# Loading padded head pairs as full 128-row tiles, with weight splits, gate transposes and the last counts in other places

## The chip, the core and the metric

The kernel runs on one core of a Trainium2 chip. A core has five engines with instruction streams of their own: TensorE (PE, matrix products; its weight loads are shown as PEld), VectorE (DVE), ScalarE (ACT), GpSimd (POOL) and SyncE (SP, which here issues DMAs), and sixteen DMA engines that move data between the device's memory and the core's on-chip memory of 128 rows (partitions). Each engine runs its instructions in order and waits where an operand or a buffer is not ready. The metric is the device time of one execution in microseconds; smaller is better.

## The reference

Two layers follow each other. The first is a gated recurrent attention (mLSTM) over 4 batches, 8 heads, 768 time steps and a head size of 40. The second is a mixture of experts: each of the 3072 tokens goes to one of 8 experts, a two-layer product of width 1024.

```python
for t in range(S):
    m_new = np.maximum(f_gate[:, :, t] + m, i_gate[:, :, t])
    f_stab = np.exp(f_gate[:, :, t] + m - m_new)
    i_stab = np.exp(i_gate[:, :, t] - m_new)
    m = m_new
    C = f_stab * C + i_stab * outer(vt, kt)
    n = f_stab * n + i_stab * kt
    h_tilde, nq = C @ qt, n . qt
    y[:, :, t] = sigmoid(o_gate) * h_tilde / max(abs(nq), 1)

logits = x @ w_gate                     # x: y as 3072 tokens of 320
expert_idx = np.argmax(logits, axis=1)  # and its softmax weight gate_w
for e in range(E):                      # the tokens of expert e
    out[mask] = gate_w[mask] * (np.maximum(x[mask] @ w1[e], 0) @ w2[e])
```

## The kernel before

**Items and steps.** The time axis is cut into 6 chunks of 128. An item is one chunk of one batch with its 8 heads: 24 items, numbered chunk by chunk (item = 4 * chunk + batch). The program is written as a hand-made order (`manual_schedule`): `start()`, then `step(s)` for s = 0 to 23, then `end()`, then the experts. Every engine runs its instructions in the order in which this code issues them. Nothing is re-ordered by a scheduler; the places of the calls set the queues.

**An attention item.** In a chunk the recurrence becomes matrix products. `scores` multiplies keys and queries (PE, L290). `spread` broadcasts the running maximum `mparts` over rows with the selector `sel` (PE, L246). `decay` makes the decay matrix `dd` on ACT (L258, eight exponentials), and POOL zeroes its upper half. `pmul` multiplies scores and decay into `pp` on DVE (L297). `attend` does the products with values: with the carried state `cz` (L310, from chunk 1 on), with `pp` (L313) and the update of the state (L317). `gated` multiplies by the sigmoid of the output gate `sg` into `yT` (DVE, L326; ACT makes the sigmoid of a whole chunk of all batches in one instruction, L212). `natural` turns `yT` to tokens in rows, together with the router's logits (PE, L345). `finish` divides and leaves the tokens `xs` (DVE, L355 to L374), and `store` writes them to device memory. `weigh_k` and `weigh_q` scale keys and queries on POOL (`kw`, `qg`), and `factors` spreads the gate factors (PE L234, ACT copy `gb` L239). In step s stand `scores(s)`, the preparation of items s+1 and s+2, `natural` and `finish` of item s-2, and `attend(s-1)`.

**Heads in rows.** Two heads share a tile of keys and queries (`tq`) or output gates (`sg`): one in rows 0 to 39, the other in rows 64 to 103. `load_t` and `load_og` fill such a tile with two DMAs of 48 rows (40 of data and 8 of padding), at rows 0 and 64. Instructions that work on all of rows 0 to 104 read the rows between as well, so POOL zeroes rows 32 to 63 of the six tiles once (L679, L708). `tq` has four buffers and is loaded three steps ahead, `sg` two.

**Gates.** The gates of all items are scanned at the start in two groups: `gt[0]` for chunks 0 to 3, `gt[1]` for chunks 4 and 5. `flip` transposes `a` (PE L193, copied by ACT to `aT`), `flip_w` makes the weights `w` (ACT, L198), transposes them (PE, L199) and copies them (`wT`). `parts` splits an f32 array in three bf16 pieces for `mparts` or `gparts`. For `gt[1]` the scan is in step 2, `carry` in step 3, the two transposes in step 4.

**Clock.** `stir` issues products of a zero tile on PE whose result nobody reads.

**Routing.** When a group of 4 or 2 items has its logits, `choose` takes the expert (DVE), `count` adds up positions with matrix products (PE, L413 to L415) in `pos_ps`, a part of the PSUM bank `x_ps` in which `natural` writes as well, `total` counts an expert's tokens (L461), `seen` reads them, `share` and `place` give weight and slot, and POOL scatters the tokens to expert lists with indirect DMAs.

**Weights.** The f32 weights of an expert come in 7 chunks, by `pull` into four buffers `raw`; `high` (ACT, L522) rounds a chunk and `low` (DVE, L526) makes the remainder. `split` does both. `SPLITS` says how many chunks are split in which step of the attention part for the first expert. `third` transposes gathered tokens (PE L561, ACT L562, DVE L564), `first` and `second` are the two layers (L576, L599).

## Time and profile before

| | |
|---|---|
| median of the runs shown | 406.84 us (404.06 to 408.29, 3 runs) |
| the profiled execution's own time | 404.99 us |
| its span, first to last instruction | 403.1 us |
| mean granted PE clock | 0.911 of full speed |
| busy: PE / PEld / DVE / ACT / POOL | 364.1 / 332.2 / 248.9 / 200.4 / 164.3 us |
| DMA | 59.01 MB, 146 GB/s over the span |
| attention part, about | 0 to 170 us |

A row of the timeline reads: start, length (us), engine, line and operation, out<-in with the shape, number of instructions merged, and in brackets the idle time of the engine before it with what ended it. Line numbers are those of the kernel before. SPq and ACTq are DMA issues. A row of the windows view has the length of the stretch, the busy time of each engine in it with the number of instructions, the granted clock of PE, the mean busy share of the sixteen DMA engines (over 1 where packets overlap) and GB/s. A row of DMA issues has the number of issues, KB of each and the median us from issue to landing.

### The profile page before, as it was taken

How to read it: one execution, taken by the hardware profiler on the slowest of the kernel's cores; microseconds unless marked ns; L12 is line 12 of the kernel's file. 1: busy time of each engine (PE TensorE's matmuls, PEld its weight loads, DVE VectorE, ACT ScalarE, POOL GpSimd, SP SyncE). 2: the span in 40 equal slices, each digit the busy share in tenths (PEclk: the TensorE clock that was granted, in tenths of full speed). 3: DMA queues.
4: the chain of work that ended last, by engine and by line, in shares of the span. 5: the costliest groups of instructions: out<-in, count | busy, mean ns of one | idle time of the engine just before them, and what ended most of it. 6: DMA issues, size and time to landing. Idle time of an engine off the chain costs nothing. (4 is left out here: it accounts for less than half of the span.)

```text
span 403.1 us, 8943 instructions
## 1 busy us (share of the span) xinstructions
PE 364.1 (90%) x3256; PEld 332.2 (82%) x3257; DVE 248.9 (62%) x625; ACT 200.4 (50%) x447; POOL 164.3 (41%) x214
## 2 busy tenths in 40 slices
PE   7788689999999987787799999999999999999970
PEld 3567678999988876687698898899999999989970
DVE  3879697999997997665352733935735556373300
ACT  3697556677765950034343533543535546454310
POOL 4726354787887575512415025014023132122020
PEclk9659696999999696589699999999999999999996
DMA  8985857798969952070742354354454545641000
GB/s 195 249 200 156 194 124 179 131 251 179 222 197 239 270 127 84 1 221 19 248 155 80 94 173 139 91 182 120 135 182 129 173 135 183 180 141 32 10 24 11
DMA packets 31535, 59.01 MB, mean 146 GB/s; under 512 B 8916, under 2 KB 20637, under 8 KB 30914
## 3 DMA queue, kind: packets, MB, share of 16 engines
q1 hardware_dynamic: 27810, 49.93, 47.8%
q0 software_dynamic: 3456, 8.36, 6.7%
q8 instruction: 26, 0.43, 0.5%
q10 hardware_dynamic: 224, 0.15, 0.1%
q14 instruction: 19, 0.16, 0.1%
HBM read 50.17 MB, written 8.70 MB: 146 GB/s over the span
## 5 line engine op out<-in xcount | busy, mean ns | idle before, releaser
L604 POOL DMA_INDIRECT out<-y,ls x24 | 23.7, 989 | 119.4 <-ACT y L603 109.1
L599 PE MATMUL bank<-w2h,hh 128*128 128x320 f32 (+1 forms) x224 | 71.1, 317 | 0.0
L586 DVE SCALAR_TENSOR_TENSOR hl<-bank,hh 128x256 fp32r<-128x256 f32 (+4 forms) x72 | 39.2, 549 | 51.4 <-ACT hh L585 50.8
L599 PE MATMUL bank<-w2h,hl 128*128 128x320 f32 (+1 forms) x224 | 69.5, 310 | 0.0
L599 PE MATMUL bank<-w2l,hh 128*128 128x320 f32 (+1 forms) x224 | 69.5, 310 | 0.0
L576 PE MATMUL bank<-xh,w1h 128*128 128x512 f32 (+4 forms) x192 | 65.4, 345 | 1.0 <-DVE xh L564 1.0
L576 PE MATMUL bank<-xh,w1l 128*128 128x512 f32 (+4 forms) x192 | 65.2, 344 | 0.0
L585 ACT ACTIVATE hh<-bank 128x256 fp32r<-128x256 f32 (+4 forms) x72 | 35.1, 488 | 46.9 <-PE bank L576 44.2
L258 ACT ACTIVATE dd<-bank,aT 128x128 f32<-128x128 f32 x192 | 52.1, 386 | 4.7 <-PE bank L246 4.5
L576 PE MATMUL bank<-xl,w1h 128*128 128x336 f32 (+4 forms) x128 | 44.0, 344 | 0.2 <-DVE xl L564 0.2
L599 PEld LDWEIGHTS bank<-w2h,hh 128*128 128x128 f32 (+1 forms) x224 | 41.4, 185 | 0.0
L599 PEld LDWEIGHTS bank<-w2l,hh 128*128 128x128 f32 (+1 forms) x224 | 41.3, 184 | 0.0
L599 PEld LDWEIGHTS bank<-w2h,hl 128*128 128x128 f32 (+1 forms) x224 | 41.2, 184 | 0.0
L603 ACT ACTIVATE y<-bank,ls 128x320 f32<-128x320 f32 (+1 forms) x24 | 12.7, 528 | 56.7 <-issue 45.4
L576 PEld LDWEIGHTS bank<-xh,w1h 128*128 128x128 f32 x192 | 36.3, 190 | 3.5 <-DVE xh L564 1.2
L576 PEld LDWEIGHTS bank<-xh,w1l 128*128 128x128 f32 x192 | 36.4, 190 | 2.3
L290 PE MATMUL bank<-tq 40*128 40x128 f32 x384 | 33.0, 304 | 4.5 <-DVE pp L297 4.2
L526 DVE TENSOR_TENSOR w1l<-raw,w1h 128x1024 fp32r<-128x1024 f32 x24 | 30.5, 1272 | 8.4 <-ACT w1h L522 8.4
L290 PEld LDWEIGHTS bank<-tq 40*128 40x128 f32 x384 | 27.6, 204 | 8.7 <-DVE pp L297 6.5
L543 POOL DMA_INDIRECT xg<-x_dram,ls x26 | 26.1, 1006 | 16.2 <-DMA ls<-lst 6.0
L297 DVE TENSOR_TENSOR pp<-bank,dd 128x512 f32<-128x512 f32 x48 | 30.8, 680 | 2.8 <-POOL dd L262 2.7
L526 DVE TENSOR_TENSOR w2l<-raw,w2h 128x640 fp32r<-128x640 f32 x32 | 26.0, 822 | 10.4 <-ACT w2h L522 9.4
(171 smaller groups left out, 694.1 us busy)
## 6 DMA issues: line engine op xcount, KB each, us to landing
raw<-in_w SPq DMA_DIRECT2D x32, 320.0 KB, 3.1
tq<-in_qk SPq DMA_DIRECT2D x48, 192.0 KB, 5.0
raw<-in_w SPq DMA_DIRECT2D x16, 512.0 KB, 3.6
tk<-in_kv SPq DMA_DIRECT2D x24, 324.0 KB, 4.9
sg<-in_og SPq DMA_DIRECT2D x12, 384.0 KB, 7.7
raw<-in_w SPq DMA_DIRECT2D x16, 256.0 KB, 3.8
x_dram<-xs SPq DMA_DIRECT2D x24, 160.0 KB, 4.7
xg<-x_dram,ls POOLq DMA_INDIRECT x26, 2.9
```

The lines of the kernel that those rows point to most:

```text
L258: nc.scalar.activation(dd[:, h, :], bc_ps[h // 4][:, h % 4], AF.Exp, bias=aT[:, c, i : i + 1], scale=-1.0)
L290: nc.tensor.matmul(s_ps[a][:, q * P : (q + 1) * P], x[r, 0, q], x[r, 1, q], start=True, stop=True)
L297: nc.vector.tensor_mul(pp[:, hs], s_ps[a].rearrange("p (q t) -> p q t", q=NP), t["dd"][:, hs])
L526: nc.vector.tensor_sub(w[name + "l"][:, c], t, f32(w[name + "h"][:, c]))
L543: nc.gpsimd.indirect_dma_start(out=xg[:T, j], out_offset=None, in_=x_dram[: 1 + items * P], in_offset=bass.IndirectOffsetOnAxis(ap=ls[:T, ...
L576: nc.tensor.matmul(ph[:, :n], a[:, k, fs], b[:, k, :n], start=not last and i == 0, stop=last and i == 2)
L585: nc.scalar.activation(hh[:, f, :n], ph[f][:, :n], AF.Relu)
L586: nc.vector.scalar_tensor_tensor(hl[:, f, :n], ph[f][:, :n], 0.0, f32(hh[:, f, :n]), ALU.max, ALU.subtract)
L599: nc.tensor.matmul(py[:T], a[:, f, ts], b[:, f], start=(f == 0 and i == 0), stop=(f == NF - 1 and i == 2))
L603: nc.scalar.activation(y[:T], py[:T], AF.Copy, scale=ls[:T, j, 2:3])
L604: nc.gpsimd.indirect_dma_start(out=out, out_offset=bass.IndirectOffsetOnAxis(ap=ls[:T, j, 1:2].bitcast(I32), axis=0), in_=y[:T], in_offset ...
```

## The change

Five edits, in one diff:

1. The host lays out keys, queries and output gates as 128 rows, 64 for each head of a pair, with zeros in rows 40 to 63 of each half (row 40 of the output gate's keeps its constant). `load_t` and `load_og` are one DMA of 128 rows each in place of two of 48, and POOL's zeroing of the rows between the heads goes.
2. At the start, `sel` is cast before `parts0` instead of after it, and four `stir` products stand before `spread(0)` instead of two. `flip_w` is cut in two: `weigh` (the exponential on ACT) and the transpose with its copy.
3. For chunks 4 and 5, `flip` moves from step 4 to step 5, behind `scores(5)`; `weigh` stands in step 5 ahead of `parts` of the gate factors; the transpose of `w` in step 6, behind `scores(6)`.
4. `SPLITS` becomes 1, 2 and 2 chunks in steps 18, 20 and 22, in place of one in each of the steps 18 to 22 and two in step 23; the remaining two chunks are split in `end()`.
5. In `end()`, `attend(23)` stands ahead of the last early count, which now uses `bank[3]` instead of `pos_ps`; `gated(23)` and `natural(22)` stand ahead of the routing of items 20 and 21.

```diff
-DR = 48
...
+    def weigh(G):
+        nc.scalar.activation(G["w"], G["a"], AF.Exp, bias=G["nm"][:, 0:1])
+
     def flip_w(G):
         n, c0 = G["n"], G["c0"]
-        nc.scalar.activation(G["w"], G["a"], AF.Exp, bias=G["nm"][:, 0:1])
         nc.tensor.transpose(gate_ps[:, P : P + n], G["w"], ident[:n, :n])
...
     def load_og(c):
-        for a in range(2):
-            nc.sync.dma_start(
-                sg[c % 2][64 * a : 64 * a + DR], og[c, a].rearrange("p (b q t) -> p b q t", b=B, q=NP)
-            )
+        nc.sync.dma_start(sg[c % 2], og[c].rearrange("p (b q t) -> p b q t", b=B, q=NP))
...
     def load_t(it):
-        for a in range(2):
-            nc.sync.dma_start(
-                tq[it % 4][64 * a : 64 * a + DR], qk[it, a].rearrange("p (k q t) -> p k q t", k=2, q=NP)
-            )
+        nc.sync.dma_start(tq[it % 4], qk[it].rearrange("p (k q t) -> p k q t", k=2, q=NP))
...
-    def count(i0, n):
+    def count(i0, n, ps=pos_ps):
...
-        rt["pos", i0] = pos = pos_ps[:, : n * E].rearrange("p (n e) -> p n e", e=E)
+        rt["pos", i0] = pos = ps[:, : n * E].rearrange("p (n e) -> p n e", e=E)
...
-    def total(items):
-
-        rt["pc", items] = pc = pos_ps[:, 4 * E : 5 * E]
+    def total(items, ps=pos_ps):
+
+        rt["pc", items] = pc = ps[:, 4 * E : 5 * E]
...
-        for t in (tq[0][32:64, 1], tq[1][32:64, 1], sg[0][32:64], tq[2][32:64, 1], tq[3][32:64, 1]):
-            nc.gpsimd.memset(t, 0.0)
...
         flip(A)
+        nc.vector.tensor_copy(sel, cs[: 3 * BH, C_SEL : C_SEL + BH])
         weave(parts0(), carry(A))
-        nc.vector.tensor_copy(sel, cs[: 3 * BH, C_SEL : C_SEL + BH])
-        stir(bank[0], 2)
+        stir(bank[0], 4)
         spread(0)
...
+        weigh(A)
         flip_w(A)
...
-        nc.gpsimd.memset(sg[1][32:64], 0.0)
...
-    SPLITS = {FIRST + 6: 1, FIRST + 7: 1, FIRST + 8: 1, FIRST + 9: 1, FIRST + 10: 1, FIRST + 11: 2}
+    SPLITS = {FIRST + 6: 1, FIRST + 8: 2, FIRST + 10: 2}
...
             pmul(s)
+        if s == 5:
+            flip(gt[1])
+        if s == 6:
+            flip_w(gt[1])
         if ok(s + 1):
...
             natural(s - 2)
-        if s == 4:
-            flip(gt[1])
-            flip_w(gt[1])
         weave(finish(s - 2) if ok(s - 2) else None)
...
         if s == 5:
+            weigh(gt[1])
             weave(parts(gt[1], "g", gparts))
...
         weights_of(NITEM - 4, 2)
-        count(NITEM - 4, 2)
-        total(MOST)
         attend(NITEM - 1)
+        count(NITEM - 4, 2, bank[3])
+        total(MOST, bank[3])
         seen(NITEM - 4, 2)
+        gated(NITEM - 1)
+        natural(NITEM - 2)
         weave(routing(NITEM - 3))
         while todo:
             scatter(todo.pop(0))
-        gated(NITEM - 1)
-        natural(NITEM - 2)
         weave(finish(NITEM - 2))
         natural(NITEM - 1)
+        split()
         third(0)
         weave(finish(NITEM - 1, late=True))
         third(1)
         weave(choose(NITEM - 2, 2))
         weights_of(NITEM - 2, 2)
         third(2)
+        split()
...
-        z = np.zeros((NCH, B, 2, DR, NP, P), a.dtype)
+        z = np.zeros((NCH, B, 2, 64, NP, P), a.dtype)
```

What this does to the queues is seen in the built programs, at two places. Line numbers of the changed kernel differ by a few; behind an underscore stands a buffer's number. First ACT in step 4 and the beginning of step 5, before. `g` are the gate factors of chunks 4 and 5, `gb_568` those spread for item 5 and `gb_660` for item 6, `dd_580` the decay of item 6, `mid` a piece of `parts`:

```order
L188 ACTIVATE g_121<-m_120,mp_124 64x128
L239 COPY gb_568<-bank_146 104x512
L258 ACTIVATE dd_580<-bank_147,aT 128x128 x4
L258 ACTIVATE dd_580<-bank_148,aT 128x128 x4
L194 COPY aT<-bank_150 128x64
L198 ACTIVATE w_122<-a_119,nm_125 64x128
L200 COPY wT<-bank_150 128x64
L171 CAST mid_127<-res_123 64x128
L175 CAST mparts<-res_123 32x128 x2
L239 COPY gb_660<-bank_146 104x512
```

And ACT now, from the copy for item 5 (`gb_554`) to the one for item 7 (`gb_752`):

```order
L234 COPY gb_554<-bank_146 104x512
L253 ACTIVATE dd_566<-bank_147,aT 128x128 x4
L253 ACTIVATE dd_566<-bank_148,aT 128x128 x4
L170 CAST mid_127<-res_123 64x128
L174 CAST mparts<-res_123 32x128 x2
L193 COPY aT<-bank_150 128x64
L234 COPY gb_641<-bank_146 104x512
L253 ACTIVATE dd_653<-bank_147,aT 128x128 x4
L253 ACTIVATE dd_653<-bank_148,aT 128x128 x4
L196 ACTIVATE w_122<-a_119,nm_125 64x128
L170 CAST mid_127<-res_123 64x128
L174 CAST gparts<-res_123 32x128 x2
```

The copy `aT`, the exponential `w` and the copy `wT` no longer stand together behind the decay of item 6: `aT` comes behind the parts, `w` behind the decay of item 7, and `wT` a further place behind what is shown.

Then PE in `end()`, before: `bank_149` holds the output of item 22 and `bank_146` that of item 23, `oh` and `ohs` are the chosen experts, `yT_2461` and `yT_last` the gated outputs of items 22 and 23:

```order
L313 MATMUL bank_149<-pp_2362,tk_2036 41x128 x8
L413 LDWEIGHTS tri
L413 MATMUL bank_151<-oh,tri 128x16
L414 LDWEIGHTS ones
L414 MATMUL bank_151<-ohs,ones 128x16
L415 LDWEIGHTS ones
L415 MATMUL bank_151<-baseb,ones 128x16
L461 LDWEIGHTS ones
L461 MATMUL bank_151<-ohs,ones 128x8
L310 MATMUL bank_146<-qg_2371,cz_143 41x128 x8
L313 MATMUL bank_146<-pp_2419,tk_2161 41x128 x8
L345 MATMUL bank_151<-cs,yT_2461 128x98 x4
```

PE now, from the end of `attend(22)` to `natural(22)`:

```order
L308 MATMUL bank_149<-pp_2326,tk_2003 41x128 x8
L305 MATMUL bank_146<-qg_2335,cz_143 41x128 x8
L308 MATMUL bank_146<-pp_2385,tk_2123 41x128 x8
L408 LDWEIGHTS tri
L408 MATMUL bank_147<-oh,tri 128x16
L409 LDWEIGHTS ones
L409 MATMUL bank_147<-ohs,ones 128x16
L410 LDWEIGHTS ones
L410 MATMUL bank_147<-baseb,ones 128x16
L456 LDWEIGHTS ones
L456 MATMUL bank_147<-ohs,ones 128x8
L340 MATMUL bank_151<-cs,yT_2425 128x98 x4
```

`attend(23)` stands ahead of the products that need the chosen experts of items 20 and 21, and these write to another bank than `natural`.

More of the change, by code (lines that the diff above doesn't have):

```diff
@@ L969, in pairs @@
     def pairs(a):
-        z = np.zeros((NCH, B, 2, DR, NP, P), a.dtype)
+        z = np.zeros((NCH, B, 2, 64, NP, P), a.dtype)
         z[:, :, :, :D] = a.reshape(B, 2, NP, NCH, P, D).transpose(3, 0, 1, 5, 2, 4)
         return z
-    qk = np.stack([pairs(k), pairs(q)], axis=4).reshape(NITEM, 2, DR, 2 * NP * P)
+    qk = np.stack([pairs(k), pairs(q)], axis=4).reshape(NITEM, P, 2 * NP * P)
     z = pairs(og)
     z[:, :, :, D] = 100.0
-    ogt = z.transpose(0, 2, 3, 1, 4, 5).reshape(NCH, 2, DR, B * NP * P)
+    ogt = z.transpose(0, 2, 3, 1, 4, 5).reshape(NCH, P, B * NP * P)
     def nat(a):
```

## The prediction

> **What bounds the kernel now.** I read the page first, then stretches by window, then the timeline where an engine stands still.
>
> ```profile
> span 403.1 us, 8943 instructions
> ...
> PE   7788689999999987787799999999999999999970
> ...
> PEclk9659696999999696589699999999999999999996
> ```
>
> ```profile
> 153.76:174.24 20.48, 15.82 (x104) 13.66 (x105) 12.94 (x51) 0.96 (x3) 9.96 (x14) 0.50 0.18 46
> 41.12:47.94 6.82, 4.41 (x49) 4.11 (x49) 3.27 (x9) 2.57 (x11) 1.54 (x2) 0.50 0.78 163
> 67.48:119.57 52.09, 51.96 (x850) 47.23 (x847) 49.09 (x164) 37.13 (x99) 43.00 (x60) 0.99 0.82 188
> ```
>
> The page's slices (10.08 us each) show PE full (9) from the seventh to the fourteenth and for most of the second half, and holes near 40 us and from 140 to 200 us. The window rows (length; busy us of PE, PEld, DVE, ACT, POOL; granted clock, DMA share, GB/s) say it in numbers: from 67.48 to 119.57, ten steps, PE works 51.96 of 52.09 us, so nothing is to be had there; in the two stretches with holes the granted clock is 0.50. The change can reach four places: the start, step 4, the arrival of the first expert weights, and the end of the attention part. The profiled execution took 404.99 us for its 403.1 us span; the median of the runs shown, 406.84, is 1.85 above it.
>
> **Start: 0.4 us.** The first `spread` (L246) opens ACT's chain of `dd`.
>
> ```profile
> 5.72 1.06 PE L665 MATMUL bank<-busy 128*128 128x512 bf16 x2
> 6.45 0.30 ACT L184 COPY mparts<-mid 32x128 bf16<-32x128 bf16 x1
> 7.66 0.17 DVE L691 CAST sel<-cs 96x32 bf16<-96x32 f32 x1
> 7.88 0.62 PE L246 MATMUL bank<-mparts,sel 96*128 96x128 bf16 x8 [1.10 <-DVE sel L691]
> 15.16 1.80 POOL L708 MEMSET sg<- 32x2048 f32 x1
> ```
>
> `sel` is cast at 7.66, though `mparts` is complete at 6.75. Cast first, it holds PE up no longer, and puts 0.17 us ahead of the parts on DVE. What comes last then are the stirs, four for two: 0.53 each (1.06/2) from 5.72 ends at 7.84, which saves nothing; if the wait ended with the second at 6.78, the 1.10 would go. I take 0.4, between 0 and 1.10. POOL's memsets, one of them 1.80 us, go; ACT's run of `dd`, sigmoid and table loads covers them, so nothing; without that cover the 1.80 would be a gain.
>
> **Step 4: 4.0 us.** Here the gate transposes of chunks 4 and 5 stand inside a step.
>
> ```profile
> 39.65 1.29 DVE L297 TENSOR_TENSOR pp<-bank,dd 128x512 f32<-128x512 f32 x2
> 40.95 2.13 ACT L258 ACTIVATE dd<-bank,aT 128x128 f32<-128x128 f32 x8
> 42.13 0.27 DVE L374 TENSOR_REDUCE lg<-pl 128x8 f32<-128x64 f32 x1
> 43.05 0.43 ACT L198 ACTIVATE w<-a,nm 64x128 f32<-64x128 f32 x1
> 43.53 0.36 PE L199 MATMUL bank<-cs,w 64*128 64x64 f32 x1 [4.35 <-ACT w L198]
> 45.81 0.69 DVE L326 TENSOR_TENSOR yT<-bank,sg 105x512 f32<-105x512 f32 x1 [3.41 <-PE bank L313]
> 46.67 0.54 DVE L169 CAST hi<-m 64x128 bf16<-64x128 f32 x1
> 50.38 1.29 DVE L297 TENSOR_TENSOR pp<-bank,dd 128x512 f32<-128x512 f32 x2
> ```
>
> PE stands 4.35 us for `w`, which ACT makes behind eight `dd`. Behind it on PE waits `attend(3)`, for whose end DVE stands 3.41 us at `gated(3)`. With the transposes gone `attend(3)` starts at about 39.2 (43.53 less 4.35) and is through before DVE has finished item 2 at 42.40; `gated(3)` follows at once: 3.41 us. Next late is DVE itself, with the `parts`: 3.71 us from 46.67 to 50.38, of which up to 1 us was spent beside POOL's work and may go. PE also sheds half-clock time, at most half of its 4.41 busy us, mostly hidden behind DVE. I take 4.0, bounds 3.4 and 5.5. The transposes themselves stay (0.36 each on PE). `a` is ready at its new place; `w` comes at the end of step 5, behind `dd(7)`, and in step 6 PE may stand some 0.5 us for it, with `factors(7)`, `spread(8)` and `attend(5)` queued behind and DVE waiting for the last. PE has slack of that size there: it stands 1.43 us for `pp` at 58.75 (below).
>
> **The loads: 1.6 us, and most in doubt.** A step of 5.21 us (52.09/10) moves, from the rows below with `sg` counted a quarter, 384+324+192+160 = 1060 KB; with 128 rows 512+324+256+160 = 1252 KB, or 1.28 MB.
>
> ```profile
> tq<-in_qk SPq DMA_DIRECT2D x48, 192.0 KB, 5.0
> raw<-in_w SPq DMA_DIRECT2D x16, 512.0 KB, 3.6
> tk<-in_kv SPq DMA_DIRECT2D x24, 324.0 KB, 4.9
> sg<-in_og SPq DMA_DIRECT2D x12, 384.0 KB, 7.7
> ...
> x_dram<-xs SPq DMA_DIRECT2D x24, 160.0 KB, 4.7
> ```
>
> ```profile
> 48.50:52.25 3.75, 3.75 (x67) 3.42 (x64) 3.57 (x10) 3.63 (x12) 0.96 (x1) 1.00 1.08 200
> ...
> 80.00:110.00 30.00, 30.00 (x501) 27.37 (x499) 28.52 (x94) 22.30 (x61) 24.88 (x39) 1.00 0.96 216
> ...
> 175.00:177.00 2.00, 0.92 (x5) 0.72 (x6) 1.24 (x7) 0.47 (x2) 0.42 (x3) 1.00 1.04 381
> ```
>
> From 48.50 to 52.25 mainly one `sg` in 48-row halves is under way: 200 GB/s with the DMA engines full. From 175 to 177 it is mainly `raw`, 128 rows of 4 KB, the form that `tq` takes on: 381 GB/s. At that rate a `tq` item takes 1.38 us (now 393 KB at 216 GB/s: 1.82) and an `sg` 2.75 (now 786 KB at 200: 3.93); with `tk` and the store at 216, 1.54 and 0.76, a step's traffic is 1.38+1.54+0.69+0.76 = 4.4 us, under 5.21, so it stays hidden. [...]
>
> ```profile
> 58.75 1.75 PE L290 MATMUL bank<-tq 40*128 40x128 f32 x16 [1.43 <-DVE pp L297]
> 128.33 1.05 ACT L522 CAST w1h<-raw 128x1024 fp32r<-128x1024 f32 x1 [4.41 <-DMA raw<-in_w]
> 129.41 1.22 DVE L526 TENSOR_TENSOR w1l<-raw,w1h 128x1024 fp32r<-128x1024 f32 x1 [2.22 <-ACT w1h L522]
> 131.29 1.75 PE L290 MATMUL bank<-tq 40*128 40x128 f32 x16 [1.27 <-DVE pp L297]
> ```
>
> The first weights are queued behind one `tq` and one `sg`, so they land 0.44+1.18 = 1.6 us earlier, and DVE's 2.22 us, ahead of `pp` and PE, shrink by that. Bounds 0 and 2.2. The splits' new steps only move pieces of 1.22 us between steps in which DVE hardly rests: nothing. The 30 DMA issues fewer on SP: nothing, since no engine waits for an issue.
>
> **The end of attention: 3.0 us.**
>
> ```profile
> 158.23 1.94 PE L313 MATMUL bank<-pp,tk 128*41 128x128 f32 x16
> 163.42 1.55 DVE L526 TENSOR_TENSOR w2l<-raw,w2h 128x640 fp32r<-128x640 f32 x2
> 164.40 0.17 PE L461 MATMUL bank<-ohs,ones 128*128 128x8 bf16 x1
> 164.50 1.93 PE L310 MATMUL bank<-qg,cz 40*41 40x128 f32 x16
> 168.23 2.03 PE L345 MATMUL bank<-cs,yT 105*128 105x98 f32 x8
> 170.30 0.17 DVE L355 TENSOR_SCALAR r<-bank 128x8 f32<-128x8 f32 x1 [1.26 <-PE bank L345]
> 171.76 1.49 PE L561 MATMUL bank<-cs,xg 128*128 128x128 f32 x6
> 172.84 0.42 DVE L564 TENSOR_TENSOR xl<-bank,xh 128x256 fp32r<-128x256 f32 x1 [0.98 <-ACT xh L562]
> ```
>
> PE is through with `attend(22)` at 160.17 and then waits for the counts. `attend(23)`, 1.93+1.94 us, now fills that wait, to 164.04. The counts end at 164.57 as before, and `natural(22)` follows there instead of at 168.23. `gated(23)` can follow the counts' reading on DVE; `natural(23)` runs on PE from 166.6 to 168.6, and the first transposes of the tokens follow, 3.1 us before their 171.76. On DVE the two `w2l` (1.55) leave the path; one returns between `finish(22)` and `xl`, where the 0.98 idle covers its 0.8. If it did not, 0.8 would be lost: bounds 2.2 and 3.6. All that follows hangs on `xl` and on the last counts, and moves with them.
>
> The sum: 0.4+4.0+1.6+3.0 = 9.0 us, so 404.99 becomes 396.0; on the median it would be 397.8. I put the forecast between the two, at 397.
>
> **Rivals.** *The extra bytes run at the old rate.* If zeros cost like data, 1.28 MB at 216 GB/s is 5.94 us a step, 0.73 over 5.21: 10.2 us in the fourteen steps from 8 to 22. The weights would land 1.8 us later ((0.262+0.131)/0.216) instead of earlier. 404.99-0.4-4.0-3.0+10.2+1.8 = 409.6, slower than before. It decides from 246 GB/s (1.28/5.21) downwards. For it speaks the DMA share of 0.96 between 80 and 110, against it 381 for this form. [...] Chance 0.10.
>
> *A new half-clock stretch.* A hole of one or two us, as before 58.75 and 131.29, moved to another phase of the step, can bring 6.82 us at half clock, as at 41.12: up to 3.4 us of PE time lost where PE sets the pace, so 399.4 to 401, more if a second follows. For it speaks that all four places shift PE's holes; against it that the middle has none. Chance 0.25.
>
> *The clock comes back sooner.* The clock is 0.50 from 153.76 to 174.24 while PE stands over 3 us near 161. Filled, that hole may let it rise for `attend(23)` and the two `natural`: half of some 4 us, less what DVE hides, about 1; and at the start up to 2 likewise. That gives 393. [...] Chance 0.15.
>
> **How the numbers follow.** The forecast has 0.50. Its own bounds give 392.6 (404.99 less 1.1+5.5+2.2+3.6 = 12.4) to 401.2 (the median less 0+3.4+0+2.2 = 5.6). To hold eight in ten the range goes from 391 to 402.5, leaving out the first rival and the worst of the second. One per cent of the median, 4.1 us, is about what a measurement of this kernel tells from no change (its three runs lie 4.2 apart). Faster by that means under 402.8: nearly all of forecast and third rival, four fifths of the second, 0.85; within 1%: 0.10; slower: half of the first rival, 0.05.
>
> **What would show it.** Right: no wait for `w` near 40 us and `pp(5)` near 46; `tq` landing well under 5.0 us and the wait for `raw` at `w1h` under 3 us; `attend(23)` ahead of the counts, the first L561-type transposes about 3 us earlier against the attention part's end. Wrong: a DMA share near 1 with PE waiting for `tq` or `tk` between 60 and 120; a step longer than 5.21 there; or new clock dips in that stretch.

## The result, and the profile after

The changed kernel takes 395.58 us (median of 4 runs, 391.69 to 396.49) against 405.45 us for the kernel before on the same chip. The ratio is 0.973, with a 95% interval of 0.966 to 0.979: faster. A second series on another chip gave 0.969 (0.956 to 0.982). The profiled execution took 394.78 us for a span of 393.0 us. The forecast was 397.0 us.

Of the kernels run further down, four were profiled in an execution over 1.5% slower than their kernel's fastest (the gate transposes alone, the changed kernel's second series, the halved loads, the old loads with stirs); from those four traces nothing is read but when the clock changes, how fast data moves, and, beside other traces that show the same, the stretch behind `yb` with its waits and gathers (below).

The page of the changed kernel, in the same parts as shown of before:

```profile
span 393.0 us, 8856 instructions
...
PE   7779799999998987795999999999999999989970
...
PEclk9859999999999798698999999999999999989996
```

PE's holes near 40 us and between 150 and 170 us are smaller, and the clock row reads 9 from 31 to 126 us, where it had two dips before. The windows say how much of that is clock. First the kernel before, then the changed one (length; busy us of PE, PEld, DVE, ACT, POOL; granted clock, DMA share, GB/s):

```profile
7.00:17.50 10.50, 8.05 (x80) 6.26 (x83) 6.49 (x14) 6.37 (x23) 5.36 (x8) 0.67 1.04 231
36.00:70.00 34.00, 27.92 (x355) 24.72 (x353) 26.86 (x83) 21.43 (x53) 14.86 (x19) 0.80 0.72 171
```

```profile
7.00:17.50 10.50, 8.07 (x96) 6.64 (x96) 7.14 (x11) 7.64 (x29) 6.33 (x12) 0.84 1.03 414
36.00:70.00 34.00, 31.25 (x492) 27.85 (x490) 31.72 (x104) 26.25 (x70) 20.23 (x26) 1.00 0.75 222
```

A mean clock of 0.80 over 34 us is 13.6 us at half speed (0.50 from 41.1 to 47.9 and from 61.6 to 68.4 us); now there are none. To place the gain, take the start of each `scores(s)` on PE in the two traces. The changed kernel is 1.1 us ahead at step 4, 6.0 at step 6, 9.0 at step 8, 7.4 at step 18, and 8.6 at step 23. Then it is 14.7 ahead at the last scatter, 13.8 at the first output `yb`, and 10.1 at the end. So the gain ran well past the forecast's 9.0 before some of it was given back.

Step 4, by the timeline of the changed kernel (`scores` is L285 there, the transposes L192 and L200, `pp` L292):

```profile
39.02 1.75 PE L285 MATMUL bank<-tq 40*128 40x128 f32 x16 [0.34 <-DVE pp L292]
41.92 0.27 PE L192 MATMUL bank<-cs,a 64*128 64x64 f32 x1 [1.15 <-DVE cz L329]
44.19 1.29 DVE L292 TENSOR_TENSOR pp<-bank,dd 128x512 f32<-128x512 f32 x2
48.36 0.24 PE L200 MATMUL bank<-cs,w 64*128 64x64 f32 x1 [1.06 <-DVE cz L332]
```

The 4.35 us for `w` is gone, and item 5's `pp` starts at 44.19 instead of 50.38. The transposes now wait at their new places, 1.15 and 1.06 us, and not for `w`: the releaser named is DVE's update of the state `cz`, which reads the PSUM bank that they write into.

The arrival of the first weights (`w1h` is L517, `w1l` L521):

```profile
119.75 1.05 ACT L517 CAST w1h<-raw 128x1024 fp32r<-128x1024 f32 x1 [3.24 <-DMA raw<-in_w]
120.83 1.86 DVE L521 TENSOR_TENSOR w1l<-raw,w1h 128x1024 fp32r<-128x1024 f32 x1 [0.99 <-ACT w1h L517]
```

Both waits are 1.2 us shorter than before (4.41 and 2.22). The end of attention (`natural` L340, `w2l` L521, the token transposes L556, their remainder `xl` L559, the first layer L571):

```profile
153.80 1.11 PE L340 MATMUL bank<-cs,yT 105*128 105x98 f32 x8
155.78 0.82 PE L556 MATMUL bank<-cs,xg 128*128 128x128 f32 x6
157.15 0.81 DVE L521 TENSOR_TENSOR w2l<-raw,w2h 128x640 fp32r<-128x640 f32 x1
157.88 0.41 DVE L559 TENSOR_TENSOR xl<-bank,xh 128x256 fp32r<-128x256 f32 x1
158.35 0.39 PE L571 MATMUL bank<-xl,w1h 128*128 128x256 f32 x1 [1.02 <-DVE w2l L521]
```

The first token transposes come at 155.78 instead of 171.76, 7.4 us sooner when measured from `scores(23)`. Behind them `w2l` stands ahead of `xl` on DVE and PE waits 1.02 us for it. What follows hangs on a chain that the prediction hadn't looked at: the last scatters into the expert lists (L450 before, L445 after), the load of the list `lsb` (L531 after), the gathers of `xgb` by POOL (L543 before, L538 after) and the transposes of `xgb` on PE. Before:

```profile
180.97 0.96 POOL L450 DMA_INDIRECT lst<-rec,slot  x1 [0.21 <-issue]
188.56 1.01 POOL L543 DMA_INDIRECT xgb<-x_dram,lsb  x1 [6.63 <-issue]
189.88 0.96 POOL L543 DMA_INDIRECT xgb<-x_dram,lsb  x1 [0.30 <-issue]
190.63 1.64 SPq L517 DMA_DIRECT2D raw<-in_w  x3
193.67 1.33 PE L561 MATMUL bank<-cs,xgb 128*128 128x128 f32 x5 [1.68 <-DMA xgb<-x_dram,lsb]
```

After:

```profile
166.29 0.96 POOL L445 DMA_INDIRECT lst<-rec,slot  x1 [0.21 <-issue]
173.78 1.63 POOL L538 DMA_INDIRECT xgb<-x_dram,lsb  x1 [6.53 <-issue]
175.29 1.64 SPq L512 DMA_DIRECT2D raw<-in_w  x3
175.72 1.49 POOL L538 DMA_INDIRECT xgb<-x_dram,lsb  x1 [0.30 <-issue]
181.58 1.33 PE L556 MATMUL bank<-cs,xgb 128*128 128x128 f32 x5 [3.61 <-DMA xgb<-x_dram,lsb]
```

The scatter is 14.7 us sooner, but POOL now takes 1.63 and 1.49 us for a gather instead of 1.01 and 0.96, so three weight loads are issued before the second gather is out (at 177.21), and PE waits 3.61 us for it. Only 12.1 us are left there. The half-clock stretch behind it is shorter than before, so `yb` is 13.8 us ahead. The last 3.7 us go in the sixth and seventh expert, where the same code waits longer for its gathered tokens and loses the clock for one window. PE's waits from `yb` on, the kernel before and the changed one (total us, times, longest):

```profile
PE bank L561 <- DMA xg<-x_dram,ls: 0.6, 2, 0.5
```

```profile
PE bank L556 <- DMA xg<-x_dram,ls: 2.2, 3, 1.1
```

From the first `yb` to the last `y` it is 180.2 us before and 183.9 after. The waits are 1.6 of these 3.7 us. Another 1.7 is half of a window at half clock, 1 us behind the longest of the waits:

```profile
348.31:351.73 3.42, 3.42 (x15) 3.42 (x14) 1.17 (x2) 0.43 (x1) 0.00 (x0) 0.50 0.22 79
```

The kernel before has the full clock from 198.1 to 396.1 us.

### The profile page after: what moved, and what is told of

Read it like the earlier page. It is cut to its first block, busy times and chain, and to the rows that moved or that the text cites. A ratio compares the mean times of both kernels' runs of the same rounds, so it can differ in the third digit from the quotient of the medians.

```text
span 393.0 us, 8856 instructions
## 1 busy us (share of the span) xinstructions
PE 357.2 (91%) x3258; PEld 327.2 (83%) x3259; DVE 246.1 (63%) x625; ACT 200.2 (51%) x447; POOL 158.8 (40%) x208
## 5 line engine op out<-in xcount | busy, mean ns | idle before, releaser
L571 PE MATMUL bank<-xh,w1h 128*128 128x512 f32 (+4 forms) x192 | 66.6, 351 | 1.2 <-DVE xh L559 1.0
L571 PE MATMUL bank<-xh,w1l 128*128 128x512 f32 (+4 forms) x192 | 66.5, 349 | 0.0
L571 PE MATMUL bank<-xl,w1h 128*128 128x336 f32 (+4 forms) x128 | 44.8, 350 | 1.6 <-DVE w2l L521 1.0
L571 PEld LDWEIGHTS bank<-xh,w1h 128*128 128x128 f32 x192 | 37.3, 195 | 3.9 <-DVE xh L559 1.2
L571 PEld LDWEIGHTS bank<-xh,w1l 128*128 128x128 f32 x192 | 37.5, 195 | 2.3
L285 PE MATMUL bank<-tq 40*128 40x128 f32 x384 | 33.1, 300 | 2.4 <-DVE pp L292 2.0
L521 DVE TENSOR_TENSOR w1l<-raw,w1h 128x1024 fp32r<-128x1024 f32 x24 | 30.8, 1289 | 7.1 <-ACT w1h L517 6.4
L257 POOL TENSOR_SCALAR_AFFINE_SELECT dd<-dd 128x1024 f32<-128x1024 f32 (+1 forms) x25 | 26.4, 1057 | 17.0 <-ACT dd L253 17.0
L285 PEld LDWEIGHTS bank<-tq 40*128 40x128 f32 x384 | 27.3, 200 | 6.7 <-DVE pp L292 4.3
L521 DVE TENSOR_TENSOR w2l<-raw,w2h 128x640 fp32r<-128x640 f32 x32 | 26.0, 822 | 10.7 <-ACT w2h L517 9.6
L292 DVE TENSOR_TENSOR pp<-bank,dd 128x512 f32<-128x512 f32 x48 | 30.9, 682 | 2.2 <-POOL dd L257 2.1
```

Of the source, the lines that this page charges most:

```text
L257: nc.gpsimd.affine_select(part, part, pattern=[[0, n], [1, P]], compare_op=ALU.is_ge, fill=0.0, base=0, channel_multiplier=-1)
L285: nc.tensor.matmul(s_ps[a][:, q * P : (q + 1) * P], x[r, 0, q], x[r, 1, q], start=True, stop=True)
L292: nc.vector.tensor_mul(pp[:, hs], s_ps[a].rearrange("p (q t) -> p q t", q=NP), t["dd"][:, hs])
L521: nc.vector.tensor_sub(w[name + "l"][:, c], t, f32(w[name + "h"][:, c]))
L571: nc.tensor.matmul(ph[:, :n], a[:, k, fs], b[:, k, :n], start=not last and i == 0, stop=last and i == 2)
```

## Experiments: each edit alone

The theory was the prediction's sum: 0.4 for the start, 4.0 for step 4, 1.6 for the loads, 3.0 for the end of attention. The rivals were that the extra bytes cost time, and that the gain is mostly granted clock. These four kernels ran on one chip, beside the kernel before (median 406.49 us, 19 runs). The new places of the splits were not tried by themselves.

**The start alone**: `sel` cast first, four stirs.

```diff
+        nc.vector.tensor_copy(sel, cs[: 3 * BH, C_SEL : C_SEL + BH])
         weave(parts0(), carry(A))
-        nc.vector.tensor_copy(sel, cs[: 3 * BH, C_SEL : C_SEL + BH])
-        stir(bank[0], 2)
+        stir(bank[0], 4)
```

> The kernel before with the start's edit alone (selector cast first, four stirs in place of two). By the prediction 0.4 us faster (0 to 1.1): the first spread at about 7.2 to 7.5 in place of 7.88, and nothing else changed. A rival is that the two stirs more move the return of the clock in the start, which would show as a full clock in the stretch from 10.4 to 13.4 and up to 1.5 us more.

Measured: 402.55 us, ratio 0.988 (0.977 to 0.998), some 5 us less, with 0.7 and 9.4 us as the ends of the interval. One row of the timeline and one of the windows:

```profile
6.92 0.62 PE L246 MATMUL bank<-mparts,sel 96*128 96x128 bf16 x8
7.00:17.50 10.50, 7.44 (x102) 5.74 (x104) 7.70 (x13) 9.00 (x32) 6.67 (x10) 1.00 1.04 216
```

The spread starts 0.96 us sooner, inside the term's bounds; but the clock in the start is 1.00 where it was 0.67, and `scores(4)` is 2.3 us sooner. The same window has 0.67 in all four traces with two stirs (before, the loads alone, the end alone, the stirs below) and 0.84 to 1.00 in the six with four. So the rival holds: the clock's part is larger than the term. Whether the stirs or the earlier `sel` bring it was not separated.

**The gate transposes alone**: `weigh` and `flip_w` cut apart, and

```diff
-        if s == 4:
-            flip(gt[1])
-            flip_w(gt[1])
+        if s == 5:
+            flip(gt[1])
+        if s == 6:
+            flip_w(gt[1])
```

> The kernel before with the gate transposes moved alone (edit 3). By the prediction 4.0 us faster (3.4 to 5.5), and the second product of scores and decay of item 5 starts near 46 in place of 50.38. By the trace of the whole change, where step 4 gives about 5 us and a half-clock stretch in step 7 is gone (2.8 us), it is up to 8 us faster. If the wait only moves to the new places, it is within 1 us of before.

Measured: 402.36 us, 4.1 us under before, but of its four runs three took 402.3 to 402.6 us and one 395.16; no interval can be given. The median lies where the prediction has it, but with a gap of 7 us within one kernel it confirms no size; something else is at play, which the next group follows.

**The end of attention alone**, with the old splits:

```diff
-        count(NITEM - 4, 2)
-        total(MOST)
         attend(NITEM - 1)
+        count(NITEM - 4, 2, bank[3])
+        total(MOST, bank[3])
         seen(NITEM - 4, 2)
+        gated(NITEM - 1)
+        natural(NITEM - 2)
         weave(routing(NITEM - 3))
         ...
-        gated(NITEM - 1)
-        natural(NITEM - 2)
```

> The kernel before with the end of the attention part in the new order alone (edit 5), all seven weight chunks still split by step 23. By the prediction 3.0 us faster at the end of the run (2.2 to 3.6). By the trace of the whole change the first token transposes come 7 us sooner against the last scores, but the layers behind wait for the expert lists: then the token transposes gain 5 us or more and the second layer's gathered tokens less than 3 us, and the run is 2 to 4 us faster. If the clock is what sets it, the stretch from 153.76 to 174.24 is at full clock for over 10 us of it.

Measured: 403.09 us, ratio 0.993 (0.988 to 0.997), 2.9 us less (1.1 to 4.7 by the interval); the term was 3.0. In its trace the first token transposes come 3.8 us sooner after `scores(23)`, not the 7.4 of the whole change, and the clock is still at half for 13.6 us between 157 and 174. The other 3.6 us in the whole change come with the other edits.

**The loads alone**: one DMA of 128 rows for two of 48, the new layout, no zeroing.

```diff
-        for a in range(2):
-            nc.sync.dma_start(
-                tq[it % 4][64 * a : 64 * a + DR], qk[it, a].rearrange(...)
-            )
+        nc.sync.dma_start(tq[it % 4], qk[it].rearrange(...))
```

> The kernel before with the 128-row loads alone (edit 1). By the prediction's term it is 1.6 us faster than before (bounds 0 and 2.2), by earlier raw weights in step 19: the first high half of w1 waits about 3.2 us for its chunk in place of 4.41. By the first rival (the extra bytes at the old rate) it is about 12 us slower. By the reading of the two traces (loads of the start over at 22 us in place of 29) something may come at the start too, up to 2 us more; then the whole is 1.2 to 3.5 us faster. The half-clock stretch at 41 us stays in every case.

Measured: 407.94 us, ratio 1.008 (1.004 to 1.012): some 3 us slower, which no theory had. The wait for the weights is 0.9 us shorter than before, in place of the 1.6:

```profile
127.89 1.05 ACT L515 CAST w1h<-raw 128x1024 fp32r<-128x1024 f32 x1 [3.51 <-DMA raw<-in_w]
...
PE bank L554 <- DMA xg<-x_dram,ls: 3.0, 3, 2.0
```

One trace doesn't size this: in the traces read for times the same wait is 3.16 us (the stirs below) to 6.34 with 48-row loads, and 1.95 to 3.51 with 128-row loads. The start gains nothing: `scores(4)` stands at 35.65 us, before at 35.56, though the loads of the start are over 7 us earlier. This trace is 1.2 us ahead of before at `yb`, and loses 4.1 us behind it, 2.4 of them in the waits of the second row and 1.7 by a window at half clock, as the changed kernel does. The first rival is refuted (a step in the middle stays at 5.10 us, between 80 and 110 us the DMA share is 0.81), but the term's sign is not borne out.

## Experiments: the clock in steps 4 to 7

Where the gate transposes are moved, PE has holes of about 1.5 us together near 40 us (0.34 and 1.15 in the rows of step 4 above). What they cost differs from nothing to 17 us at half clock.

**Stirs in steps 4 to 7**, on the kernel before with the gate transposes moved. The added products keep PE at work in the hole:

```diff
+        if 4 <= s <= 7:
+            stir(gb_ps, 3)
         if s == 5:
             flip(gt[1])
```

> The kernel before with the gate transposes moved (edit 3 alone) and three products of the zero tile more in each of the steps 4 to 7, ahead of the next item's factors, where PE has waits of about a microsecond. They add 12 times 0.27 us of PE work at full clock. If the half-clock stretch that follows PE's holes there (43 to 60 us in the run of edit 3 alone) is what the steps 5 and 6 lose, it goes or is under 4 us long, scores(8) starts near 61 in place of 65.48, and the run takes 397 to 399. If DVE alone sets these steps, the products cost their own time or nothing: 402 to 405.

Measured: 399.46 us against 407.75 before, ratio 0.977 (0.971 to 0.982).

```profile
36.00:70.00 34.00, 33.26 (x499) 28.33 (x495) 31.78 (x102) 27.10 (x71) 20.59 (x26) 1.00 0.82 184
```

No half clock from 31.5 to 127 us, and `scores(8)` at 59.73. With 48-row loads, work that computes nothing brings these steps to the pace that the changed kernel has (58.50): the half clock, which lasts from 42.8 to 59.8 us where the transposes are moved without the stirs, is what was lost there.

**The changed kernel with the old loads.**

```diff
-        nc.sync.dma_start(tq[it % 4], qk[it].rearrange(...))
+        for a in range(2):
+            nc.sync.dma_start(tq[it % 4][64 * a : 64 * a + DR], qk[it, a].rearrange(...))
```

> The changed kernel with the loads of 48 rows and POOL's zeroing put back (edit 1 undone, edits 2 to 5 kept). By the prediction's term it is 1.6 us slower than the changed kernel (397.2 against 395.6). If the loads cost by themselves, as their run alone suggests (407.9 against 406.5), it is 1 to 3 us faster than the changed kernel (393 to 395). If the changed kernel's full clock from 31 to 126 us hangs on the shorter loads of the start, it is 3 to 7 us slower (399 to 403), with a half-clock stretch of 7 us or more between 40 and 70.

Measured: 393.56 us, ratio 0.964 (0.960 to 0.967), the lowest of all kernels run. Its trace nevertheless has 17 us of half clock between 40 and 57 us, and `scores(8)` only at 62.76; at `yb` it is 4.5 us behind the changed kernel, and makes 3.7 of that good behind `yb`, where it takes 180.2 us.

**The old loads from the new layout**: as above, but the arrays in memory have 64 rows per head, of which the DMAs take 48.

```diff
+            nc.sync.dma_start(tq[it % 4][64 * a : 64 * a + DR], qk[it, a, :DR].rearrange(...))
```

> The changed kernel with the old loads (two DMAs of 48 rows, POOL's zeroing), but with the arrays in device memory laid out as 128 rows, of which the DMAs take 48 in 64. It tells the place of the data in memory from the form of the loads. In traces with 128-row loads the stretch from the first yb to the last y takes 183.9 to 185.1 us, with 48-row loads 180.2 to 182.1. If the larger arrays (other addresses for all that follows) make the gathers late, it is over 183 here; if the form or the number of the DMAs does, it is 180 to 182. The time by the first case 395 to 398, by the second 392 to 395.

Measured: 403.53 us against 407.00 before (394.12 to 409.1, six runs; no interval). From `yb` to the last `y` 183.9 us, with 48-row loads and the old number of DMAs; so neither the form of the loads nor their number decides that loss. That the layout does is what this pair of kernels would say; the next kernel, with 183.9 in the old layout, speaks against it. Behind `yb` the two traces part in the seventh expert, where POOL issues a gather (L545) at nearly the moment at which DVE begins a remainder `w1l` (L528). The old loads first, then the new layout:

```profile
343.93 0.95 POOL L545 DMA_INDIRECT xg<-x_dram,ls  x1 [3.20 <-PE bank L578]
343.99 1.23 DVE L528 TENSOR_TENSOR w1l<-raw,w1h 128x1024 fp32r<-128x1024 f32 x1 [0.43 <-ACT w1h L524]
```

```profile
344.06 1.22 DVE L528 TENSOR_TENSOR w1l<-raw,w1h 128x1024 fp32r<-128x1024 f32 x1 [0.43 <-ACT w1h L524]
344.17 1.94 POOL L545 DMA_INDIRECT xg<-x_dram,ls  x1 [3.38 <-PE bank L578]
351.92 0.45 PE L563 MATMUL bank<-cs,xg 112*128 112x112 f32 x1 [2.06 <-DMA xg<-x_dram,ls]
```

Begun 0.06 us ahead of the remainder, the gather takes 0.95 us; begun 0.11 behind it, 1.94. The next gather is then issued 1.1 us behind a weight load instead of 0.06 ahead of it, PE waits 2.06 us for the last gather, and a window at half clock follows (351.9 to 355.3 us), which the first trace does not have.

In steps 4 to 7 these two kernels, which differ only in where the data lies, part ways. In these traces the changes of the clock lie whole multiples of 3.41 us apart, so the windows are cut at this beat; the old loads first, then the new layout, then the changed kernel:

```profile
36.65:40.06 3.41, 2.27 (x38) 1.77 (x34) 3.24 (x11) 3.40 (x10) 2.00 (x2) 0.99 1.18 158
40.06:43.48 3.42, 2.87 (x19) 2.76 (x20) 3.31 (x10) 2.95 (x12) 1.23 (x1) 0.50 1.05 253
```

```profile
37.81:41.23 3.42, 2.77 (x48) 2.27 (x44) 3.16 (x12) 3.39 (x9) 1.77 (x2) 1.00 1.10 152
41.23:44.64 3.41, 2.30 (x29) 2.14 (x31) 3.12 (x9) 1.96 (x9) 1.37 (x2) 1.00 0.87 258
44.64:48.05 3.41, 3.41 (x46) 2.88 (x40) 2.96 (x10) 2.97 (x11) 0.00 (x0) 0.50 1.11 229
```

```profile
37.71:41.13 3.42, 2.62 (x46) 2.11 (x40) 3.21 (x12) 3.39 (x10) 1.86 (x2) 1.00 1.06 215
41.13:44.54 3.41, 2.62 (x35) 2.46 (x37) 3.30 (x9) 2.93 (x12) 1.37 (x2) 1.00 0.93 311
44.54:47.95 3.41, 2.76 (x56) 2.32 (x50) 3.27 (x12) 1.91 (x8) 1.60 (x2) 1.00 0.96 335
```

In the first two kernels a window with PE busy for 2.27 and for 2.30 us is followed by half clock; in the changed kernel the hole falls across two windows of 2.62 us each, and the clock stays. At this place, in these three traces, the drop goes with how the hole lies to the windows. Between 20 and 75 us in ten traces (all but the four named under the result), nine of the ten windows at full clock just ahead of a drop had PE busy for under 2.4 us, and all but one of the 98 that kept the clock for over 2.5. Later no single bound sorts the windows (in the start's run one with 1.84 us busy kept the clock at 190 us and one with 3.03 lost it at 136), and why the first kernel stays at half for five windows, the last four with PE busy throughout, while the second returns after one, is open.

**The old loads with the stirs.**

```diff
+        if 4 <= s <= 7:
+            stir(gb_ps, 3)
```

> The changed kernel with the old loads (48 rows) and three products of the zero tile more in each of the steps 4 to 7. If the 128-row loads help the attention part only by keeping PE's holes short enough in steps 4 to 7 that the clock stays up, the stirs do the same: the half-clock stretch from 40 to 57 us goes, scores(8) starts near 59 in place of 62.76, and with the shorter layers behind it is 3 us faster than the kernel without stirs, 389 to 392. If the loads help in another way, it is at 393 or above.

Measured: 397.56 us, ratio 0.970 (0.960 to 0.980), the same as the changed kernel beside it (0.969). The stretch at half clock between 40 and 57 us is gone, as expected, but the 3 us are not gained. The stretch behind `yb` is 183.9 us here, with old loads and old layout.

**The changed kernel once more**, on the chip of the last two, with no edit.

> The changed kernel once more, on the chip of the three runs beside it. By its first result 0.973 of the time before. If the earlier gap between it and the kernel with 48-row loads (0.9727 against 0.9637) was the chip or chance, it is within 0.5% of that kernel here, too. The stretch from the first output yb to the last output y, where no load of keys and queries runs, was 183.87 us in its first trace, against 180.21 before; if that is the loads' doing it stays above 183.

Measured: 397.68 us against 407.00, ratio 0.969 (0.956 to 0.982), with single runs from 390.59 to 405.67. Its second trace has half clock from 42.5 to 45.9 us, behind the same wait of 1.15 us that cost nothing in the first. The old loads' 0.964, from another chip, lies inside this interval, and its two nearest relatives (403.53 and 397.56) did not repeat it. So no kernel here is shown to beat the changed one.

**Each 128-row load as two DMAs of 64 rows**, with the same bytes:

```diff
-        nc.sync.dma_start(tq[it % 4], qk[it].rearrange(...))
+        for a in range(2):
+            rows = slice(64 * a, 64 * a + 64)
+            nc.sync.dma_start(tq[it % 4][rows], qk[it, rows].rearrange(...))
```

> The changed kernel with each 128-row load issued as two DMAs of 64 rows: the bytes of the change, but the number of DMAs of the kernel before. If the late gathers come from the number of DMAs that went before, the stretch from the first yb to the last y falls to 180 to 182 us; if from the bytes or the layout, it stays above 183. For the attention part: if one DMA over all 128 rows is what makes the loads fast, the start is as slow as before (loads over at about 29 us, a half-clock stretch of 7 us or more between 40 and 60); if the bytes per row or the two halves side by side do, the loads are over by 24 us.

Measured: 400.14 us, ratio 0.986 (0.978 to 0.993). The start's loads, in the kernel before, in the changed kernel, and then in halves:

```profile
2.00:12.00 10.00, 7.66 (x45) 4.01 (x43) 4.92 (x17) 5.03 (x16) 4.04 (x6) 0.92 1.02 224
12.00:20.00 8.00, 6.50 (x65) 4.82 (x65) 6.80 (x7) 5.15 (x20) 6.28 (x10) 0.67 1.04 271
```

```profile
2.00:12.00 10.00, 8.77 (x55) 5.05 (x55) 5.50 (x18) 5.85 (x20) 1.99 (x3) 0.92 0.99 372
12.00:20.00 8.00, 5.86 (x67) 4.19 (x64) 6.83 (x8) 6.30 (x20) 6.12 (x10) 0.89 1.04 416
```

```profile
2.00:12.00 10.00, 9.22 (x80) 5.44 (x79) 5.72 (x19) 6.76 (x23) 1.99 (x3) 1.00 0.97 231
12.00:20.00 8.00, 4.85 (x44) 3.00 (x44) 5.88 (x8) 7.25 (x17) 4.38 (x8) 0.92 1.03 257
```

231 to 257 GB/s in halves, 372 to 416 in one piece, with the DMA engines full in both (shares of 0.97 to 1.04). What makes the change's loads fast is that one DMA spans all 128 rows; a pair that covers the same rows is no faster than the kernel before (224 to 271 GB/s). From `yb` to the last `y` it takes 183.9 us, as with the new layout in the other forms.

## Experiments: what the end's gain was given back to

**The remainders made later**: on the changed kernel, the two last `w2l` behind the token transposes.

```diff
-        split()
+        high(loaded[0])
         third(0)
         ...
         third(2)
+        low(loaded.pop(0))
         split()
```

> The changed kernel, with only the order in its end changed: the remainders of the last two weight chunks are made behind the third transposition of the tokens, where the changed kernel makes the first of them ahead of it (its rounding on ACT stays where it was). If the remainder w2l stands on the path, as the trace of the changed kernel reads (the first product with xl waits 1.02 us behind it), that wait falls under 0.5 and the second layer's first output comes 1 us sooner, and 2 to 3 us sooner if the half-clock stretch from 160.5 to 167.5 goes with it. If the layers behind wait for the expert lists in any case, the run is within 1 us of the changed kernel (394.6 to 396.6).

Measured: 399.41 us against 407.75, ratio 0.983 (0.976 to 0.989). PE no longer waits for `w2l`, and the first output of the second layer comes at 172.00 instead of 174.38 us. But `yb` does not move:

```profile
197.09 0.53 ACT L598 ACTIVATE yb<-bank,lsb 128x320 f32<-128x320 f32 x1 [3.08 <-PE bank L594]
```

The changed kernel has it at 197.08. Both had their last scatter at 166.3 to 166.5 us, and PE's first transposes of `xgb` stand at 177.45 and 177.64: there the chain over the lists takes PE's gain. The second ones come 1.9 us sooner (179.67 instead of 181.58), after gathers of 0.97 and 0.96 us and a wait of 1.90, but PE is then at half clock for 6.8 us (178.4 to 185.2) where the changed kernel is for 3.4. So lists and clock together leave `yb` where it was. The third case of the expectation holds for the step, not for the time, which lies above its 394.6 to 396.6. The run is not faster, so this 1.02 us is no loss of the whole.

**The lists earlier**: the last count, slots, scatters and list loads inside the first slice of the first layer, the last store ahead of the weight loads, and the remainders late.

```diff
+            if key == "a" and f == 0:
+                after(-1)
             products(f, ph[f], True)
...
-            if f == 0:
-                weave(share(NITEM - 2, 2))
-            if f == 1:
+            if f == -1:
                 count(NITEM - 2, 2)
+                weave(share(NITEM - 2, 2))
...
         store(NITEM - 2)
+        store(NITEM - 1)
         expert(1)
```

> The changed kernel with three edits behind the attention part: the last remainders made later (as in the run beside it), the last count, its slots, scatters and the loads of the next two lists brought forward from behind the second slice of the first layer to inside the first slice, and the store of the last item ahead of the loads of the second expert's weights. If what the tail's gain was given back to is the chain from the last slots over the lists to the gathered tokens (3.61 us of wait for xgb at 181.58, with a half-clock stretch behind it), the last scatters start near 162 in place of 165.01, that wait goes under 1 us, and the run takes 390 to 393. If the gather is late for another reason (it shares the DMA engines with the weight loads), the wait stays over 2 us and the run is within 1.5 us of the changed kernel.

Measured: 397.39 us, ratio 0.970 (0.962 to 0.978): not the 390 to 393. The scatters did not come near 162:

```profile
161.72 1.56 DVE L521 TENSOR_TENSOR w2l<-raw,w2h 128x640 fp32r<-128x640 f32 x2
164.28 0.17 DVE L438 CAST slot<-ss 128x2 int32<-128x2 f32 x1
164.73 0.98 POOL L445 DMA_INDIRECT lst<-rec,slot  x1 [2.91 <-DVE slot L438]
```

The remainders, put late, now stand on DVE ahead of the slots, and the scatter starts at 164.73 instead of 165.01. PE's wait for the second gather of `xgb` fell from 3.61 to 1.66 us, between the two cases of the expectation, behind gathers of 0.98 and 0.96 us; half clock from 178.7 to 185.5 us follows, and `yb` comes at 197.72. The edit missed its aim for the scatters, so what an earlier scatter is worth was not tested by it.

## Why the prediction was right, and where it was not

The sum was 9.0 us; the medians differ by 9.9 and the two profiled executions by 10.2. It is right in total and in half of its terms; two errors of opposite sign met, so that the total came this near is in part luck. By their own runs start, step 4, loads and end give about 5.0, 4.1 (without an interval), -3.2 and 2.9 us.

**Start, 0.4: too small.** The spread moved by 0.67 us, within the bounds; the four stirs took 1.65 us (1.24 in the run alone), not 0.53 each. What the term left out is the clock: the half-clock stretch of 6.8 us in the start is gone or 3.4 us long, and alone the edit is worth 0.7 to 9.4 us. The third rival had named "at the start up to 2 likewise", which is what `scores(4)` shows in the run alone (2.3).

**Step 4, 4.0: right in kind, and low.** The wait for `w` went, DVE's `pp(5)` came 6.2 us sooner, 5.1 of them from this step, within the bounds. The wait predicted at the new place (0.5 us for `w`) came as waits for `cz`, 1.15 and 1.06. And 3.0 us more came by step 8, as the half-clock stretch from 61.6 to 68.4 went; no term had that.

**Loads, 1.6: this is the term that failed.** What it counted on did come: 372 to 416 GB/s where it took 381, a wait for the weights shorter by 0.9 to 1.2 us, steps in the middle of 5.10 us with PE busy throughout; only steps 11 and 17 are longer than before, by 0.7 and 1.3 us in the changed kernel (0.6 and 0.0 with the loads alone). At 5.96 and 6.72 us they are the steps longer than 5.21 that the prediction listed as a sign of being wrong; but PE waits for no load in them, and what lengthens them stays open. But `tq` did not land "well under 5.0 us": in the loads' run the median from issue to landing is 5.2 us, for 512 KB instead of 192, and the wait at `w1h` is 3.24, not under 3. The 0.9 us do not reach the end; the loads alone are 0.8% slower. In the run's trace the loss lies behind `yb` (4.1 us), where the edit has no instruction.

**End of attention, 3.0: right alone (2.9).** In the whole change the step gave 7.4 us at the token transposes. Two of its sentences failed. "The 0.98 idle covers its 0.8" did not: PE waits 1.02 us behind `w2l`. "All that follows hangs on `xl` and on the last counts, and moves with them" did not either: it hangs on the scatters, which gained 6.1 us over `scores(23)`, and on the gathers behind them, which gave 0.9 back by `yb`.

**Splits, nothing:** they cost that 1.02 us, which does not show in `yb`.

**Rivals.** The extra bytes did not run at the old rate: 372 to 416 GB/s in the start's loads where it was 224 to 271, and a DMA share of 0.81 between 80 and 110 us with the loads alone where it was 0.96. A new half-clock stretch came in the changed kernel's second trace (42.5 to 45.9) and not in its first; the clock came back sooner in its first (at half for 3.4 and 6.8 us between 150 and 168 us, where it was for 20.5 from 153.8 on). One kernel shows both, so these two were not rivals so much as the spread of one distribution, and the range was rightly wide enough for them.

No term had the loss of 3.7 us behind `yb`. It is 180.2 to 182.1 us in six of the traces (before, the start, the end and the transposes alone, the transposes with stirs, the changed kernel with the old loads) and 183.9 to 185.1 in eight; all that have the 128-row layout in memory are among the eight, but so is one with the old layout, and the old form and number of loads stand on both sides. In all of them the code is the same there. The parts add up: PE's waits for gathers are 0.5 to 2.3 us in the six and 2.2 to 3.5 in the eight, and each of the eight, but none of the six, has one window of 3.41 us at half clock, 150 to 152 us behind `yb`. Without these waits and half of that window, all fourteen take 179.6 to 180.2 us.

What sorts the waits is the order of one gather and one remainder, in the two traces shown above and in the rest: in five of the six the first gather of the seventh expert begins 0.02 to 0.28 us ahead of `w1l`, takes 0.95 us, and no wait there is over 0.7; in the transposes with stirs and in seven of the eight it begins 0.1 to 0.9 us behind, takes 1.1 to 1.95, and PE waits 1.8 to 2.1 us. The changed kernel's first trace lies between (0.02 us behind, 0.95, a wait of 1.05). So a tenth of a microsecond seems to decide. That is read from the traces; no run set this order by hand, and why the traces with the new layout fall on the late side, the changed kernel's first just so, is open.

## What to carry to other kernels

Price a hole on TensorE twice: by its own length, and by the clock windows behind it; a hole of about 1.5 us cost between nothing and 17 us at half clock here, and in both traces that had them a few products of zeros in the hole left no half clock there. When a chain at the end of a phase is shortened, follow each of its outputs (here the expert lists, not the matrix products) to its next reader before counting the gain. Load a tile of 128 rows with one DMA, even if a third of it is zeros: 372 to 416 GB/s in the start here, against 231 to 257 with two DMAs of 64 rows. But don't count time for it where the transfers were hidden: alone these loads made the kernel 0.8% slower. Where a loss moves between kernels with the same code, look for two instructions on different engines that start at nearly the same moment: here a tenth of a microsecond between a gather and a subtraction goes with 2 us of wait.

## What the runs showed of the hardware

**The clock changed on a beat of 3.41 us.** In the trace before, the granted clock changes at 10.4, 17.2, 20.6, 30.9, 41.1, 48.0, 61.6 and 68.4 us: gaps of 2, 1, 3, 3, 2, 4 and 2 times 3.41 us. The other traces that were cut this way have the same beat with another offset: what is left of these times after division by 3.41 is 0.1 to 0.3 us before, 2.7 to 2.8 in the start's run, 2.4 to 2.6 with the old loads, and 0.1 to 0.2 and 1.4 to 1.6 in the two traces of the changed kernel. The stretches at half clock in steps 4 to 7 alone are 0 to 17 us, and single runs of the changed kernel lie between 390.59 and 405.67 us.

**Gathers on POOL that begin while DVE makes a remainder took longer.** In ten traces (all but the four named under the result) POOL issues 280 gathers of `xg` and `xgb`. Of these, 27 begin while DVE is already making a remainder `w1l` or `w2l` that has more than 0.2 us to go. They end 0.82 to 0.89 us after the remainder does, and so take 1.07 to 1.95 us; the two of `xgb` in the changed kernel (1.63 and 1.49) are among them. The 240 that begin outside a remainder take 0.93 to 1.02 us. Two more begin within 0.02 us of a remainder's start: they take 0.95 and 0.93, and there the remainder takes 1.27 and 1.26 us instead of 1.22 or 1.23. No run changed this order alone.
